# Two channels in one matmul for half of the kernel products, rows of group 2 copied earlier, and six tile stores moved to another queue

## The chip, the cores and the metric

The kernel runs on one core of a Trainium2 chip. A core has five engines with one instruction queue each: TensorE (PE) for matmuls, VectorE (DVE) and GpSimd (POOL) for elementwise work, ScalarE (ACT) for activations and copies, SyncE (SP) for issuing DMAs; ACT and POOL issue DMAs too. Matmuls write to PSUM, everything else lives in SBUF or in DRAM. The metric is the device time of one execution in microseconds, as the median of several runs.

## The reference, cut to what matters

A block of a network over 2048 tokens of 576 channels: a layer norm with modulation, a long convolution over the tokens (S4D), a second layer norm with modulation, and a feed-forward layer of 4608 hidden units. The convolution's filter K is itself computed, from 128 complex modes for each channel:

```
dt = exp(log_dt);  A = -exp(log_A_real) + 1j * A_imag;  C = (C_real + 1j * C_imag) * dt
P  = exp((A * dt)[:, :, None] * pos[None, None, :])
K  = 2 * einsum("dn,dnl->dl", C, P).real
y  = irfft(rfft(u, 2L) * rfft(K, 2L), 2L)[:L] + u * D_skip
x  = x + ga * y(layernorm(x) * (1 + ca) + sa)
x  = x + gb * (relu(h2 @ w1) @ w2),  h2 = layernorm(x) * (1 + cb) + sb
```

`sa, ca, ga, sb, cb, gb` are six vectors of `silu(c) @ w_mod`. All is float32.

## The kernel before, in words

The tokens are taken in four blocks of 512. The feed-forward part (`ffn`) runs block after block and takes most of the time; while PE works on one block there, the filter, the transforms and the norm of the next block are put between its matmuls, from generators. The change lies ahead of the first matmul of `ffn`, where the first block (block 0) is prepared and nothing of the feed-forward part can run yet.

**The filter for block 0.** `KGen.first` computes it in six groups of 96 channels, each group as two halves `u` of 48. The 512 taps are split in 32 positions `j` and 16 offsets `a`: `values` makes a table `W2` over the 32 positions (cosines and sines on ACT, multiplications on DVE and POOL, in `half_values`), `start` makes the first column of `W1`, `doubling` fills its 16 columns in four steps, and `products` multiplies: for each channel one pair of matmuls (real and imaginary part, `r`) with the 128 modes as rows, the 32 positions as weights and the 16 offsets as moving columns. Four channels (`dd`) go to the four strips of 32 PSUM partitions; 48 channels and 2 parts make 96 matmuls for each half, 192 for each group. A float32 matmul stands in the trace as two records, so a group has 384 of them (L264). `powers` makes the factors `Z` that the doubling uses.

**Rows.** `rows(g)` copies a group's products from PSUM to `ke` (one ACT copy of 128 x 384); after three groups `store` writes `ke` to DRAM (`kd`), and `load_kt` reads it back in another layout (`kt`). Group 2 completes the first half of the channels (p = 0), group 5 the second (p = 1). `src_K` adds `D_skip` to the first tap, on one partition of `kt` (on DVE for p = 0, on POOL for p = 1).

**What orders the work.** A scheduler orders each engine's queue at build time, by program order and readiness. Instructions that go through `act` and `pool` of `KGen` (all of its ACT work and nearly all of its POOL work), and through `kept` once `pinned` is set, keep their program order on their engine. In `first` the loop over `g in (0, 2)` has: `raw` (exponentials and turns), doubling and products of groups g and g+1, values of group g+2, then values of group g+3, between the two halves of which `rows(g)` and the first two doubling steps of group g+2 run. After the loop the generator hands over to `conv0` and is taken up again from there for groups 4 and 5.

**The transforms of block 0.** `conv0` has, in this order: the transform of the input half p = 0 (`ZU`, 8 matmuls of 288 columns), the transform of the filter half p = 0 (`ZK`) interleaved with the products of group 4, the doubling and products of group 5, then on DVE the butterflies of U and K, the product Y and the first inverse butterfly V; on PE meanwhile the transform of the input half p = 1, then inverse transforms (L1025), the transform of the filter half p = 1 (`transform1`, L801 and L803, which does the first butterfly on PE with negated constants in 16 matmuls), and the modulation products; then Y and the inverse for p = 1, the norm, and `ffn`. `early` holds the transform constants `fcu` and `fck`; `fcU`, `fcK` and `gc` are tiles of 4 KB a partition in pools that open when those of the first stage close.

**Stores for later blocks.** `W1`, `W2` and `Z` of each half group are also stored to DRAM, for the taps of the later blocks. `values` and `double` issue these on SP, except for group 5 and for `W1` of group 4: those are put in `k.held` and issued on POOL in `conv0`, two behind the load of the modulation weights for sb and cb (L1180), the other six behind that for gb (L1225). Each `W2` tile has 128 x 3072 floats, each `W1` tile 128 x 1536, each `Z` tile 128 x 192.

## Time and profile before

| | us |
|---|---|
| median of 3 runs | 1343.76 |
| lowest and highest | 1338.28 and 1344.12 |
| the profiled execution | 1342.5 |
| its span, first to last instruction | 1340.7 |

| engine | busy us | share of the span |
|---|---|---|
| PE | 1218.8 | 91% |
| DVE | 869.8 | 65% |
| ACT | 504.2 | 38% |
| POOL | 195.2 | 15% |

The profile is one execution. A timeline row has the start and the length in us, the engine (PE for matmuls, PEld for weight loads, SPq for the queue of SP), the line of the kernel, the operation, the written tile and the read ones, partitions x elements, how many instructions were merged, and in brackets how long the engine had been idle before and what released it ("issue" where it waited for nothing that the profile shows). A row of the windows has the length of the stretch, the busy time of each engine with its number of instructions, TensorE's granted clock (1.00 is full), the share of time that the DMA engines were busy, and GB/s. A row of the chain of waits has the start, the length and what the end was waiting for. Durations of merged rows run from the first start to the last end.

### The profile page before, as it was taken

What the parts mean: (1) busy time and instruction counts of PE and PEld (TensorE: products, weight loads), DVE (VectorE), ACT (ScalarE), POOL (GpSimd) and SP (SyncE); (2) the same over time, 40 slices, a digit from 0 to 9 for tenths busy, and PEclk for the clock granted to TensorE, in tenths of its full rate; (3) what the DMA queues carried; (4) which work ended last, traced back from release to release, by engine and by line L of the source; (5) the groups of instructions that cost most, each with busy time, mean ns of one, the idle gap of its engine ahead of it and who ended that gap; (6) DMA issues with size and microseconds to landing.
All of it is one profiled execution on the core that took longest, in us unless ns stands there. A gap on an engine that the chain in (4) does not pass through costs nothing.

```text
span 1340.7 us, 26038 instructions
## 1 busy us (share of the span) xinstructions
PE 1218.8 (91%) x10608; PEld 972.3 (73%) x10608; DVE 869.8 (65%) x1351; ACT 504.2 (38%) x1014; POOL 195.2 (15%) x271
## 2 busy tenths in 40 slices
PE   5125699899999998999999999999999999999998
PEld 3124567678787786777777786787888888888886
DVE  5998898999887898289447885366988222111111
ACT  7987124222224323522243225343322353232331
POOL 1788131111120000111101100100010000000000
PEclk9555799899999998999999999999999999999999
DMA  6666499888898876698779893758997556666651
GB/s 199 246 248 248 145 362 407 303 281 302 293 357 283 291 253 209 222 384 309 245 255 332 289 372 117 264 182 275 318 348 237 169 178 213 196 199 200 196 168 62
DMA packets 132424, 340.47 MB, mean 254 GB/s; under 512 B 22352, under 2 KB 22672, under 8 KB 132304
## 3 DMA queue, kind: packets, MB, share of 16 engines
q1 hardware_dynamic: 105200, 215.21, 48.7%
q0 software_dynamic: 26816, 123.01, 25.1%
q8 instruction: 83, 1.36, 0.4%
q10 hardware_dynamic: 288, 0.59, 0.1%
q14 instruction: 37, 0.30, 0.1%
HBM read 258.55 MB, written 80.22 MB: 253 GB/s over the span
## 4 chain that ended last, share of the span: by engine, by line
PE 71%; DVE 12%; DMA 8%; issue 6%; POOL 2%; ACT 2%; SPq 0%; DVEq 0%; ACTq 0%; POOLq 0%
PE hps L1334 28%; PE acc L1359 27%; PE kps L445 5%; PE ps_f L764 3%; DVE T L515 3%; DVE Y L515 3%; DMA Ua<-Ud 3%; PE kps L264 2%; PE ps_i L1025 2%; DVE W L515 1%; PE kps L612 1%; DMA Ka<-Rd 1%; DMA Zr<-Zd 1%; DMA wm_gb<-in_w_mod_dram 1%; POOL W L59 1%
## 5 line engine op out<-in xcount | busy, mean ns | idle before, releaser
L1359 PE MATMUL acc<-hh,w 128*128 128x512 f32 x1296 | 422.2, 400 | 2.1 <-DVE w L515 2.0
L1334 PE MATMUL hps<-xh,w 128*128 128x512 f32 x1152 | 395.0, 403 | 0.7 <-ACT xh L1090 0.4
L1359 PEld LDWEIGHTS acc<-hh,w 128*128 128x128 f32 x1296 | 243.4, 189 | 55.3 <-DVE w L515 2.8
L1359 PE MATMUL acc<-hl,w 128*128 128x512 f32 x720 | 281.1, 400 | 0.0
L1340 DVE SCALAR_TENSOR_TENSOR hl<-hps,hh 128x512 fp32r<-128x512 f32 x144 | 98.9, 687 | 278.1 <-ACT hh L1339 277.8
L1334 PEld LDWEIGHTS hps<-xh,w 128*128 128x128 f32 x1152 | 218.1, 190 | 48.6 <-ACT xh L1090 1.8
L1334 PE MATMUL hps<-xl,w 128*128 128x512 f32 x576 | 230.7, 401 | 0.2 <-DVE xl L1095 0.2
L1339 ACT ACTIVATE hh<-hps 128x512 fp32r<-128x512 f32 x144 | 86.2, 598 | 328.4 <-PE hps L1334 323.8
L1312 ACT ACTIVATE w<-r 128x576 fp32r<-128x576 f32 x144 | 98.8, 687 | 237.8 <-issue 183.1
L1359 PEld LDWEIGHTS acc<-hl,w 128*128 128x128 f32 x720 | 135.8, 189 | 28.3
L1334 PEld LDWEIGHTS hps<-xl,w 128*128 128x128 f32 x576 | 109.4, 190 | 25.1 <-DVE xl L1095 1.5
L1305 ACT ACTIVATE w<-r 128x640 fp32r<-128x640 f32 x142 | 103.9, 732 | 16.7 <-DMA r<-in_w_dram 15.9
L264 PE MATMUL kps<-W,W 128*32 128x16 f32 x2304 | 40.1, 217 | 76.0 <-POOL W L59 46.9
L1334 PE MATMUL hps<-xs,w 128*128 128x512 f32 x288 | 97.7, 419 | 2.2 <-DVE hl L1340 2.0
L264 PEld LDWEIGHTS kps<-W,W 128*32 128x32 f32 x2304 | 37.7, 150 | 80.5 <-POOL W L59 48.1
L515 DVE TENSOR_TENSOR Y<-Y,T 128x1152 f32<-128x1152 f32 x64 | 85.0, 1352 | 0.1
L445 PEld LDWEIGHTS kps<-W1r,W2r 128*32 128x32 f32 x3456 | 63.8, 146 | 27.9 <-issue 21.6
L445 PE MATMUL kps<-W1r,W2r 128*32 128x48 f32 (+2 forms) x3456 | 71.3, 237 | 8.4 <-issue 7.3
L765 ACT ACTIVATE Z<-ps_f 128x288 f32<-128x288 f32 x104 | 42.4, 408 | 64.5 <-PE ps_f L764 62.3
L1334 PEld LDWEIGHTS hps<-xs,w 128*128 128x128 f32 x288 | 53.7, 192 | 15.0 <-DVE hl L1340 3.1
L515 DVE TENSOR_TENSOR W<-Z 128x576 f32<-128x576 f32 x52 | 37.0, 754 | 40.6 <-ACT Z L765 40.6
L515 DVE TENSOR_TENSOR w<-r,w 128x512 fp32r<-128x512 f32 (+2 forms) x108 | 58.0, 573 | 3.3 <-ACT w L1312 3.0
(215 smaller groups left out, 1361.9 us busy)
## 6 DMA issues: line engine op xcount, KB each, us to landing
r<-in_w_dram SPq DMA_DIRECT2D x144, 320.0 KB, 4.1
r<-in_w_dram SPq DMA_DIRECT2D x144, 288.0 KB, 3.7
w<-L1d SPq DMA_DIRECT2D x108, 320.0 KB, 3.0
w<-L2d SPq DMA_DIRECT2D x108, 288.0 KB, 3.1
W2r<-W2d POOLq DMA_DIRECT2D x18, 1536.0 KB, 9.2
W2d<-W SPq DMA_DIRECT2D x10, 1536.0 KB, 7.4
W<-W1d POOLq DMA_DIRECT2D x18, 768.0 KB, 9.2
Ua<-Ud POOLq DMA_DIRECT2D x12, 1152.0 KB, 10.4
```

Source lines behind the costliest of these rows:

```text
L264: self.nc.tensor.matmul(ps[32 * dd : 32 * dd + 32, 12 * u + q, :], W2[:, r, :, ch], W1[:, u, :, r, ch], start=(r == 0), stop=(r == 1),)
L445: nc.tensor.matmul(ps[32 * dd : 32 * dd + 32, q, :], W2[:, r, :, ch], W1[:, :na, r, ch], start=(r == 1), stop=(r == 0),)
L515: return self.kept(self.nc.vector.tensor_tensor(*args, **kw))
L764: kept(nc.tensor.matmul(o, fc[:, n2, c, :], src(n2), start=True, stop=True))
L765: nc.scalar.activation(Z[:, n2, c], ps[:, :PC], AF.Copy)
L1025: self.nc.tensor.matmul(ps[:, :PC], a, b, start=(i == 0), stop=(i == len(todo) - 1))
L1305: nc.scalar.activation(w[:, 0], r, AF.Copy)
L1312: nc.scalar.activation(w[:, 0:D], r2[g], AF.Copy)
L1334: nc.tensor.matmul(ps, a, x, start=(i == 0), stop=(i == 13))
L1339: nc.scalar.activation(hh, ps, AF.Relu)
L1340: nc.vector.scalar_tensor_tensor(hl, ps, 0.0, hh, op0=ALU.max, op1=ALU.subtract)
L1359: nc.tensor.matmul(acc[i], a, x, start=(f == 0 and j in (0, 3, 6, 9, 12)), stop=(f == NF - 1 and j in (2, 5, 8, 11, 13)),)
```

## The change

- **Products of groups 3 to 5** go through a new method, `pairs`: one matmul takes two channels (`x`), so 64 weight columns (32 positions of two channels) and 32 moving columns (16 offsets of two channels). Of the four blocks that come out, the two that mix channels are not used. A group has 96 matmuls in place of 192 and fills both PSUM banks. `rows` copies each half on its own, and `ke` gets a second plane for the channel of the pair; the rows that belong together lie on every fourth partition, and the store of p = 1 becomes four DMAs, two each on SP and ACT.
- **Rows of group 2** are copied and stored inside the values of group 4 (`ahead`), together with the loads of `fcu` and `fck`; the products of group 3 come behind the values of group 4. `kt` for p = 0 (`kt0`) is loaded inside the values of group 5 (`head`), into the slot of `cc`.
- **Stores.** Those of `W2` and `Z` of group 4 come behind that load, and the six held stores at hand after the doubling of group 4 (`W2` and `Z` of group 5, `W1` of group 4) are issued on SP there; only the two of `W1` of group 5 are left for POOL.
- **Skip addition.** `D_skip` is laid out in a tile `skip` by three small DMAs at the start and added to `ke` before the store, in place of `kt` after the load.
- **U transform for p = 0**: `transform1` with negated constants (`fcUn`, a new load on SP into `fcU`) in place of `transform` and `butterfly1`.
- **Places**: `gcn`, `cb` and `row` go into unused halves of `fcK` and `fcU`.

```diff
--- before.py
+++ after.py
@@ -83,9 +83,15 @@
         self.a, self.th = (self.pa.tile([P, D], F32, name=n) for n in ("lar", "th"))
         ai = self.pt.tile([P, D], F32, tag="T1", bufs=2, name="ai")
         dt = self.pt.tile([P, D], F32, tag="T0", bufs=2, name="dt")
-        self.cc = pc.tile([P, 2, D], F32, name="cc")
+        self.cc = pc.tile([P, 2, D], F32, tag="cc", bufs=1, name="cc")
         self.halfpi = pc.tile([P, 1], F32, name="halfpi")
         nc.vector.memset(self.halfpi, math.pi / 2)
+        self.skip = pc.tile([P, 2, 72], F32, name="skip")
+        nc.gpsimd.memset(self.skip, 0.0)
+        dv = I["dsk"].rearrange("(dd p q) -> p dd q", dd=4, p=2)
+        nc.gpsimd.dma_start(out=self.skip[::32, 0], in_=dv[0])
+        for x in range(2):
+            nc.gpsimd.dma_start(out=self.skip[x::64, 1], in_=dv[1, 2 * x : 2 * x + 2])
         nc.sync.dma_start(out=dt, in_=I["ldt"].unsqueeze(0).to_broadcast([P, D]))
         nc.scalar.dma_start(out=ai, in_=I["ai"])
         nc.scalar.dma_start(out=self.a, in_=I["lar"])
@@ -270,6 +276,26 @@
                         )
                     )
 
+    def pairs(self, banks, W1, W2s, between):
+
+        for u in range(2):
+            a = W2s[u].rearrange("p r j (x c) -> p r (j x) c", x=2)
+            b = W1[:, u].rearrange("p a r (x c) -> p r c x a", x=2)
+            for q in range(12):
+                if q % 6 == 3:
+                    for _ in range(2):
+                        next(between, None)
+                for r in range(2):
+                    for half in range(2):
+                        c = 12 * half + q
+                        o = banks[u][64 * half : 64 * half + 64, 32 * q : 32 * q + 32]
+                        self.mm = self.kept(
+                            self.nc.tensor.matmul(
+                                o.rearrange("p (x a) -> p x a", x=2), a[:, r, :, c], b[:, r, c],
+                                start=(r == 0), stop=(r == 1),
+                            )
+                        )
+
     def first(self, setup, mod, norm):
 
         nc, k = self.nc, self.k
@@ -306,15 +332,22 @@
             self.half_values(g, W2, E[2:4], F[0], True)
             then()
             self.half_values(g, W2, E[0:2], F[1], False)
+            if g != 4:
+                saves(g, 0)
+            self.powers(g, E[4], F[2])
+            if g != 4:
+                saves(g, 1)
+
+        def saves(g, i):
             for u in range(2):
-                save(
-                    strips(k.W2d[2 * g + u], 4),
-                    W2[u].rearrange("p r (y b) c -> p (r y) (b c)", y=2), g == NG - 1,
-                )
-            self.powers(g, E[4], F[2])
-            zs = self.Z[g][1]
-            for u in range(2):
-                save(k.Zd[2 * g + u], zs[:, :, :, u * H : u * H + H], g == NG - 1)
+                if i:
+                    zs = self.Z[g][1]
+                    save(k.Zd[2 * g + u], zs[:, :, :, u * H : u * H + H], g == NG - 1)
+                else:
+                    save(
+                        strips(k.W2d[2 * g + u], 4),
+                        W2s[g][u].rearrange("p r (y b) c -> p (r y) (b c)", y=2), g == NG - 1,
+                    )
 
         def double(g, steps=range(4)):
             self.doubling(g, steps)
@@ -328,17 +361,58 @@
 
         def multiply(g, between=iter(())):
             self.kept = k.kept if g == NG - 2 else lambda x: x
+            if g > 2:
+                kps[g] = [self.bank() for _ in range(2)]
+                self.pairs(kps[g], self.W1[g], W2s[g], between)
+                return
             kps[g] = self.bank()[:, :384].rearrange("p (q a) -> p q a", a=16)
             for u in range(2):
                 self.products(kps[g], self.W1[g], W2s[g][u], u, between)
 
         def rows(g):
             if g % 3 == 0:
-                ke[0] = self.pc.tile([P, 16, 72], F32, tag="ke", bufs=1, name=f"ke_{g}")
-            qs = slice(24 * (g % 3), 24 * (g % 3) + 24)
-            self.act(ke[0][:, :, qs], kps.pop(g).rearrange("p q a -> p a q"), AF.Copy)
-            if g % 3 == 2:
-                self.store(0, g // 3, ke[0].rearrange("p a q -> p (a q)"), nc.sync)
+                ke[0] = self.pc.tile([P, 2, 16, 72], F32, tag="ke", bufs=1, name=f"ke_{g}")
+            t = ke[0]
+            q0 = 24 * (g % 3)
+            if g < 3:
+                self.act(t[:, 0, :, q0 : q0 + 24], kps.pop(g).rearrange("p q a -> p a q"), AF.Copy)
+            else:
+                for u, ps in enumerate(kps.pop(g)):
+                    self.act(
+                        t[:, :, :, q0 + 12 * u : q0 + 12 * u + 12],
+                        ps[:, :384].rearrange("p (q x a) -> p x a q", x=2, a=16), AF.Copy,
+                    )
+            if g == 2:
+                nc.vector.tensor_tensor(t[:, 0, 0], t[:, 0, 0], self.skip[:, 0], op=ALU.add)
+                self.store(0, 0, t[:, 0].rearrange("p a q -> p (a q)"), nc.sync)
+            elif g == 5:
+                nc.gpsimd.tensor_tensor(
+                    t[:, :, 0], t[:, :, 0],
+                    self.skip[:, 1].unsqueeze(1).broadcast_to([P, 2, 72]), op=ALU.add,
+                )
+                f = t.rearrange("p x a q -> p x (a q)")
+                for y in range(2):
+                    for x, eng in enumerate((nc.sync, nc.scalar)):
+                        k.kept(eng.dma_start(
+                            out=k.kd[0][1][64 * y + 32 * x : 64 * y + 32 * x + 32],
+                            in_=f[2 * y + x :: 4, x],
+                        ))
+
+        def ahead():
+            rows(2)
+            t = k.early = self.pc.tile([P, 2, 4, 2, P], F32, tag="W1", bufs=4, name="early")
+            for i, n in enumerate(("fcu", "fck")):
+                nc.sync.dma_start(out=t[:, i], in_=k.I[n])
+
+        def head(g):
+            if g == 0:
+                rows(0)
+            double(g + 2, range(2))
+            if g == 2:
+                k.kt0 = self.pc.tile([P, 16, 72], F32, tag="cc", bufs=1, name="kt0")
+                nc.sync.dma_start(out=k.kt0, in_=k.kd_rows(0, 0))
+                for i in range(2):
+                    saves(4, i)
 
         load, stats, scale, center, affine = norm
         next(mod)
@@ -352,28 +426,31 @@
         values(1, lambda: None)
         for g in (0, 2):
             raw(g // 2 + 1)
-            for i in (g, g + 1):
-                double(i, range(2, 4) if i == 2 else range(4))
-                multiply(i)
-            values(g + 2, lambda: None)
-            if g == 2:
-                t = k.early = self.pc.tile([P, 2, 4, 2, P], F32, tag="W1", bufs=4, name="early")
-                for i, n in enumerate(("fcu", "fck")):
-                    nc.sync.dma_start(out=t[:, i], in_=k.I[n])
-            values(g + 3, lambda: (rows(g), double(g + 2, range(2))))
+            double(g, range(2, 4) if g else range(4))
+            multiply(g)
+            double(g + 1)
+            if g == 0:
+                multiply(1)
+            values(g + 2, ahead if g else lambda: None)
+            if g:
+                multiply(3)
+            values(g + 3, lambda: head(g))
             rows(g + 1)
             if g == 0:
                 for i in (2, 3):
                     affine(i)
         yield
         double(4, range(2, 4))
+        for dst, src in k.held:
+            k.kept(nc.sync.dma_start(out=dst, in_=src))
+        k.held.clear()
         between = yield
         multiply(4, between)
         yield
         double(5)
         yield
+        rows(4)
         multiply(5)
-        rows(4)
         rows(5)
 
     def store(self, s, p, ke, eng):
@@ -615,7 +692,9 @@
 
         nc, act = self.nc, lambda *a, **kw: self.kept(self.nc.scalar.activation(*a, **kw))
         cv = self.cv
-        cb = cv.tile([P, 5, 32], F32, name="cb")
+        spare = self.fcU[:, 2:].rearrange("p a b c -> p (a b c)")
+        cb = spare[:, : 5 * 32].rearrange("p (k r) -> p k r", k=5)
+        row = spare[:, 256:]
         self.kept(nc.vector.tensor_copy(cb, self.ct.unsqueeze(2).broadcast_to([P, 5, 32])))
         ws = {}
 
@@ -643,7 +722,6 @@
                 load(5, "gb")
             elif nm == "gb":
                 yield
-            row = cv.tile([P, 2 * P], F32, tag="row", bufs=1, name=f"row_{nm}")
             act(row[:, 0:P], ps[:, 0:P], AF.Copy)
             for o in (P, P + 64):
                 act(row[0:32, o : o + 64], ps[0:32, P : P + 64], AF.Copy)
@@ -1111,10 +1189,8 @@
         cpsa = self.cps, self.nps = self.pool(c, "cpsa", space=PSUM), 2
         cpsa = cpsa[0]
         self.half_tag = "kt"
-        self.dsk = self.fcU[0:1].rearrange("p a b c -> p (a b c)")[:, :D]
-        nc.gpsimd.dma_start(out=self.dsk, in_=I["dsk"].unsqueeze(0))
-        fcKn = self.fcK.rearrange("p a b c -> p (a b) c")[:, 0:4]
-        gcn = cva.tile([P, 4, P], F32, name="gcn")
+        fcUn, fcKn = (t.rearrange("p a b c -> p (a b) c")[:, 0:4] for t in (self.fcU, self.fcK))
+        gcn = self.fcK.rearrange("p a b c -> p (a b) c")[:, 4:]
         self.pinned = True
 
         def behind(d, op):
@@ -1128,18 +1204,16 @@
             return self.kept(nc.sync.dma_start(out=t, in_=a))
 
         early = self.early
-        kt = [self.load_kt(0, 0)]
+        load(fcUn, I["neg"][2])
+        kt = [self.kt0]
         hv = self.h.rearrange("m n (dd p q) -> m n dd p q", dd=4, p=2)
 
         def src_K(p):
             ktv = kt[p].rearrange("p (t dd g) q -> p t dd g q", t=2, g=2)
-            dv = self.dsk.rearrange("o (dd p q) -> o dd p q", dd=4, p=2)[:, :, p]
-            add = nc.gpsimd.tensor_tensor if p else self.v
-            add(ktv[0:1, 0, :, 0], ktv[0:1, 0, :, 0], dv, op=ALU.add)
             return lambda n2: ktv[:, n2 // 2, :, n2 % 2]
 
-        ZU, ZK = S(0, "ZU"), S(1, "ZK")
-        run(self.transform(lambda n2: hv[:, n2, :, 0], early[:, 0], ZU))
+        WU, ZK = S(2, "WU"), S(1, "ZK")
+        run(self.transform1(lambda n2: hv[:, n2, :, 0], early[:, 0], fcUn, WU))
         next(first)
         ZKs = self.transform(src_K(0), early[:, 1], ZK, self.kept)
         first.send(ZKs)
@@ -1149,10 +1223,8 @@
             behind(d, kg.mm)
         next(first)
         kg.factors.close()
-        W = S(2, "W")
-        run(self.butterfly1(ZU, W))
         U0 = S(0, "U0")
-        run(self.butterfly2(W, U0, -1))
+        run(self.butterfly2(WU, U0, -1))
         self.save(self.Ud[0][0], U0)
         W = S(3, "W")
         run(self.butterfly1(ZK, W))
@@ -1261,13 +1333,13 @@
         self.pinned = False
         self.half_tag = "T"
 
+    def kd_rows(self, s, p):
+        kd = self.kd[s][p]
+        return bass.AP(tensor=kd.tensor, offset=kd.offset, ap=[[72, P], [9216, 16], [1, 72]])
+
     def load_kt(self, s, p):
         kt = self.cv.tile([P, 16, 72], F32, tag="kt", bufs=1 if s else 2, name="kt")
-        kd = self.kd[s][p]
-        d = (self.nc.gpsimd if s else self.nc.sync).dma_start(
-            out=kt,
-            in_=bass.AP(tensor=kd.tensor, offset=kd.offset, ap=[[72, P], [9216, 16], [1, 72]]),
-        )
+        d = (self.nc.gpsimd if s else self.nc.sync).dma_start(out=kt, in_=self.kd_rows(s, p))
         if s == 0:
             self.ktd = self.kept(d)
         return kt
@@ -1565,7 +1637,8 @@
     r["gc"] = (np.stack([np.cos(ps), -np.sin(ps)], axis=2) / 512).astype(np.float32)
     r["neg"] = -np.stack(
         [r["fck"][:, 2:].reshape(P, 4, P),
-         np.stack([r["gc"][:, n, c] for n, c in ((1, 0), (2, 0), (2, 1), (3, 1))], axis=1)]
+         np.stack([r["gc"][:, n, c] for n, c in ((1, 0), (2, 0), (2, 1), (3, 1))], axis=1),
+         r["fcu"][:, 2:].reshape(P, 4, P)]
     )
     sg = 1.0 - 2.0 * (j % 2)
     r["sgn"] = np.stack([sg, -sg], axis=1).astype(np.float32)
```

## The prediction

> **What bounds the kernel now.** I read the windows first, to see where TensorE is full.
>
> ```profile
> core 0: us, PE busy (x) PEld busy (x) DVE busy (x) ACT busy (x) POOL busy (x), PEclk, DMA share, GB/s
> ...
> 150.00:200.00 50.00, 41.05 (x631) 31.44 (x625) 47.57 (x74) 12.63 (x32) 13.62 (x17) 0.90 0.88 320
> ...
> 350.00:400.00 50.00, 50.00 (x913) 40.96 (x912) 39.13 (x60) 13.00 (x27) 10.92 (x17) 1.00 0.87 316
> ...
> 1200.00:1250.00 50.00, 50.00 (x222) 41.38 (x222) 5.54 (x8) 15.15 (x24) 0.00 (x0) 1.00 0.66 198
> ```
>
> From 350 us on PE has work nearly all the time at full clock, and the change leaves the feed-forward part alone. So the end is the moment at which that part starts plus a constant, and a microsecond won ahead of it is a microsecond of the whole. The timeline gives its first matmul.
>
> ```profile
> 209.46 1.20 PE L1334 MATMUL hps<-xs,w 128*128 128x512 f32 x2
> ```
>
> The diff works between 100 and 200 us. There I followed DVE in the timeline, since from 150 on it is busy 47.57 of 50 us.
>
> ```profile
> 129.96 3.54 DVE L515 TENSOR_TENSOR T<-W,Zp 128x768 f32<-128x768 f32 x4
> 138.66 0.45 DVE L515 TENSOR_TENSOR kt<-kt,fcU 1x288 f32<-1x288 f32 x1 [5.16 <-DMA kt<-kd]
> 139.03 0.34 DVE L515 TENSOR_TENSOR t<-W,Zp 128x192 f32<-128x192 f32 x1
> ...
> 149.79 2.76 DVE L515 TENSOR_TENSOR W<-ZU 128x576 f32<-128x576 f32 x4
> 152.58 2.90 DVE L515 TENSOR_TENSOR U<-W 128x576 f32<-128x576 f32 x6
> 155.40 2.76 DVE L515 TENSOR_TENSOR W<-ZK 128x576 f32<-128x576 f32 x4
> ...
> 168.99 2.77 DVE L515 TENSOR_TENSOR V<-Y 128x576 f32<-128x576 f32 x4
> ```
>
> From 138.66 to 171.8 DVE runs almost without a pause: skip addition, doubling of group 5 (139.03 to 149.8), butterflies of U and K, product, V. The 5.16 us ahead of it are a wait for the load of `kt`: a load that is late, not an engine that is full. The chain of waits agrees; it stays on DVE until V and hands over to PE there.
>
> ```profile
> 171.14 3.18 PE ps_i L1025 x12
> ```
>
> The load is late because its store is late: SP stores `kd` only at 125.53, behind four tile stores and `fck`.
>
> ```profile
> 112.14 0.88 SPq L362 DMA_DIRECT2D early<-in_fcu_dram  x1
> 117.72 2.36 SPq L298 DMA_DIRECT2D W2d<-W  x2
> 120.86 2.56 SPq L298 DMA_DIRECT2D Zd<-zs  x2
> 123.47 1.97 SPq L362 DMA_DIRECT2D early<-in_fck_dram  x1
> 125.53 1.97 SPq L382 DMA_DIRECT2D kd<-ke  x2
> ```
>
> **The change, part by part.** *Rows of group 2 forward.* The rows are PE's, ACT's, DVE's and POOL's in the timeline, then the landing times of `kd`, then two windows.
>
> ```profile
> 109.63 2.15 PE L264 MATMUL kps<-W,W 128*32 128x16 f32 x127 [1.83 <-issue]
> ...
> 125.42 1.80 PE L264 MATMUL kps<-W,W 128*32 128x16 f32 x99 [4.62 <-issue]
> ```
> ```profile
> 112.32 0.92 ACT L56 ACTIVATE c<-c,halfpi 128x768 f32<-128x768 f32 x1
> ...
> 125.47 0.44 ACT L56 ACTIVATE zs<-c,halfpi 128x192 f32<-128x192 f32 x1
> ```
> ```profile
> 120.44 0.34 DVE L180 TENSOR_TENSOR tc<-cc,s 128x192 f32<-128x192 f32 x1
> ```
> ```profile
> 115.68 1.85 POOL L59 TENSOR_TENSOR W<-c,E 128x384 f32<-128x384 f32 x2
> ...
> 128.68 1.15 POOL L59 TENSOR_TENSOR zs<-zs,E 128x192 f32<-128x192 f32 x2
> ```
> ```profile
> DMA to landing us min/median/max: 3.6/5.0/6.9
> ```
> ```profile
> 110.00:120.00 10.00, 5.25 (x334) 5.03 (x329) 6.93 (x20) 7.60 (x15) 10.00 (x15) 0.50 0.73 269
> 120.00:130.00 10.00, 5.38 (x159) 4.14 (x152) 9.48 (x28) 5.17 (x11) 10.00 (x16) 0.56 1.00 350
> ```
>
> The products of group 2 end near 111.3, 98 records into the burst of 109.63. Copied and stored at once, `kd` is in memory by about 118. `kt0` takes the slot of `cc`, whose last reader runs at 120.44, so it is issued near 121.5 and there by 127, over 11 us ahead of 138.66. The 5.16 us go, and what is late next is DVE itself, at 133.5 after its four T. The ACT copy now stands in ACT's fixed order inside group 4's values and waits for 111.3; queued behind it are abs, two sines and the cosine that POOL uses at 115.68 (done at 113.2). I estimate 1.2 us of delay, hidden by POOL's own queue, full from 110 to 130; without that cover it costs up to 1.2.
>
> *Skip addition.* The 0.45 us on DVE go. Two additions over 128 partitions come, one on DVE between 110 and 120 (busy 6.93 of 10), one on POOL (0.57 us by the zs row) in the path to `kt1`. POOL's old 2.08 us at 173 lay beside PE. The memset and the three small loads stand at the start, where POOL idles.
>
> *U transform.* It now does the first butterfly too: 32 matmul records for 16, and the 2.76 us of DVE go.
>
> ```profile
> 127.16 5.83 PE L764 MATMUL ps_f<-h,early 128*128 128x288 f32 x16
> ```
> ```profile
> 174.31 0.48 PE ps_f L801 x2
> ```
>
> Between 16 records in 5.83 us at this place and 0.24 us each in the K1 transform, 32 cost 7.8 to 11.7; I take 9.5, in the middle. PE starts about 126, when ACT's last reading of the factor tiles under the target ends (125.47 + 0.44), and is done at 135.5.
>
> *Paired products.* A group costs 192 records in place of 384. Unpaired ones start every 17 ns (127 in 2.15 us), and after some 128 PE stands still for 1.8 to 4.6 us waiting for nothing that the profile shows, which I read as instructions not yet there: a block each 4.0 us. A paired record has 64 weight and 32 moving columns; no row shows it.
>
> ```profile
> 237.65 2.31 PE L445 MATMUL kps<-W1r,W2r 128*32 128x48 f32 x96
> ```
> ```profile
> 143.00 1.24 PE L764 MATMUL ps_f<-kt,early 128*128 128x288 f32 x4
> ...
> 162.93 0.42 PE L264 MATMUL kps<-W,W 128*32 128x16 f32 x6 [2.12 <-issue]
> ```
> ```profile
> 173.22 2.08 POOL L1138 TENSOR_TENSOR kt<-kt,fcU 1x288 f32<-1x288 f32 x1 [11.07 <-DMA kt<-kd]
> ```
>
> Below it are the 17 ns; the nearest row, 32 weight and 48 moving columns, has 24 ns, and two of those, 48 ns, do more than one paired record, so that is the upper end. I take 30 ns, 5.8 us a group, nearer to the row than to its double, and keep both ends.
>
> [...]
>
> Group 4 with the K transform in it: 5.8 + 4 times 1.24 + some 0.5 for switching = 11.3 us, from 135.5 to 146.8, K's last copy near 146.5. DVE doubles group 5 from 133.5 (10.8 us as before) to 144.3 and makes U0 until 147.1. So K is there in time, by half a microsecond. Group 5: 5.8 us and one standstill of 2 to 154.6. Before, products ended at 163.35 and `kt1` came 9.9 us later; with POOL's addition 10.5, so 165.1. The K1 transform, at 174.3 before, could start 8.4 earlier, at 165.9. That just fits too. The second ACT copy of a group adds 0.48 us where ACT is a quarter busy.
>
> *Six stores moved.* Two W2 tiles (1.6 MB each), two Z tiles and two W1 tiles (0.8 MB each) leave POOL, where they were issued from 177 to 199, for SP after 129. 4.9 MB at the 350 GB/s of 120 to 130 last 14 us. The W1 stores wait for POOL's doubling of group 4; queued behind them are constants that wait for the products of group 4 anyway, then half of the `kd` rows, `kt1` and x, none due before 150. On POOL the stores stood around the load for gb, and PE waited for it.
>
> ```profile
> PE kps L445 <- issue: 4.3, 3, 2.5
> ...
> PE mps_gb L638 <- DMA wm_gb<-in_w_mod_dram: 0.5, 1, 0.5
> ```
>
> They also ran beside loads at the head of the feed-forward part; PE loses a few microseconds there, by these waits of 200 to 330 with other causes, so I count zero and keep 3 us either way.
>
> **Sum.** 5.16 + 0.45 + 2.76 = 8.4 us on DVE's chain, 0.5 at gb, less 0.9 for the two fits without slack: 8.0. The profiled execution took 1342.5 us (span 1340.7 and 1.8 around it), 1.3 below the median 1343.76 and inside the runs. 1342.5 - 8.0 = **1334.5 us**.
>
> **Rivals.** *The U transform waits.* Its negated constants are new on SP. Queued behind group 4's stores, which start near 122 and take 9.5 us for 3.3 MB, they land at 133, not 126: U ends at 142, K at 153.5, and DVE's 155.40 becomes 153.9. Gain 1.5 + 0.5: 1340.5 us. For: SP issued `fck` behind just these stores. Against: their tile lies on inputs that are read last near 104, and `fcu` went ahead of the stores.
>
> *Paired records cost more.* At the upper end, 48 ns, groups 4 and 5 cost 9.2 us each, but a block then lasts longer than the 4.0 us in which one comes, and the standstill goes: products end at 159.4, `kt1` comes at 169.9, 4.0 later than it could be used: 1342.5 - 8.9 + 4.0 = 1338 us. [...]
>
> *Slower: PE starves beside the stores.* The longest standstill, 4.62 us, fell where W2 stores ran and DMA was full. Now 4.9 MB run beside groups 4 and 5. U late by 6.5, two standstills 2.6 us longer and 384 records at 48 ns (6.9 us) move the end of products from 154.6 to 173.2, `kt1` to 183.7, 9.4 behind 174.3: 1352 us. It is slower than before once products end after 164, by over 0.5% from 170.5.
>
> *It moves nothing*, since the queues keep their order: 1342.5. *More than forecast*: DVE's wait for products of group 3 goes as well (1.9) and the head of the feed-forward part loses 3 less: 1329.
>
> ```profile
> 119.50 0.56 DVE L173 TENSOR_TENSOR W<-s,E 128x384 f32<-128x384 f32 x1 [1.93 <-PE kps L264]
> ```
>
> **How the numbers follow.** Forecast 0.46 (1331 to 1337), more 0.12, late U 0.20, dear pairs 0.14, nothing 0.03, starved PE 0.05. About 0.5%, 6.7 us, is what a measurement of this kernel can tell from no change: faster is below 1337.0, slower above 1350.5. Faster: 0.46 + 0.12 + 0.02 of the dear pairs = 0.60; slower 0.05; same 0.35. The range goes from 1327 (more, with 2 us of spread) to 1342.5 (late U with 2 us); the starved case and the tails are left out.
>
> **What would show it.** Right: no DVE wait on `kt`; U0's butterfly starts by 145; V ends near 163.5; `kt1` lands by 166; the first L1334 matmul is at 201.5, not 209.46. Late U: PE pauses inside the U transform for a load of `fcU`. Dear pairs: 192 records last over 8 us without a standstill. Starved: standstills over 4 us from 135 to 155. I am wrong as a whole if the feed-forward part starts 8 us earlier and the end does not follow.

## The result, and the profile after

| | median, us | lowest to highest | runs | ratio to before, 95% interval |
|---|---|---|---|---|
| before | 1341.24 | 1338.28 to 1344.12 | 8 | 1 |
| after | 1352.74 | 1345.30 to 1357.54 | 8 | 1.0078 [1.0052, 1.0103] |

The change makes the kernel slower; 1334.5 us was forecast, with 1327.0 to 1342.5 as the range. The profiled execution of after took 1351.98 us (span 1350.2).

The timeline of after on PE, around the changed work (start, duration, engine, line, names, shape, count, in brackets the idle time ahead and its releaser). Its lines moved: L293 holds the paired products, L270 the unpaired ones, L879 and L881 the transform with the first butterfly, L842 the K transform, L1406 the feed-forward part.

```profile
112.22 12.38 PE L293 MATMUL kps<-W,W 128*64 128x32 f32 x192
...
133.95 0.45 PE L293 MATMUL kps<-W,W 128*64 128x32 f32 x4 [3.41 <-POOL W L59]
134.91 1.48 PE L293 MATMUL kps<-W,W 128*64 128x32 f32 x20 [0.52 <-POOL W L59]
136.32 2.29 PE L881 MATMUL ps_f<-h,fcU 128*128 128x288 f32 x4
...
143.43 0.65 PE L881 MATMUL ps_f<-h,fcU 128*128 128x288 f32 x2
...
145.26 3.24 PE L293 MATMUL kps<-W,W 128*64 128x32 f32 x48
148.43 2.24 PE L842 MATMUL ps_f<-kt,early 128*128 128x288 f32 x4
150.60 3.26 PE L293 MATMUL kps<-W,W 128*64 128x32 f32 x48
...
164.33 12.38 PE L293 MATMUL kps<-W,W 128*64 128x32 f32 x192
...
188.47 0.72 PE L879 MATMUL ps_f<-kt,early 128*128 128x288 f32 x2 [3.02 <-DMA kt<-kd]
...
224.39 0.73 PE L1406 MATMUL hps<-xs,w 128*128 128x512 f32 x2 [0.29 <-DVE xs L1171]
```

A group of 192 paired records lasts 12.38 us: 64.5 ns a record, where the forecast took 30 and its upper bound was 48. No `issue` stands between them, so the standstills have gone; the records fill the time instead. The price is the same at both clocks: 48 records take 3.24 us from 145.26 and 3.26 us from 150.60, where the windows (busy time by engine, then the granted clock, DMA share and GB/s) give 1.00 and 0.50:

```profile
145.30:148.30 3.00, 3.00 (x49) 3.00 (x48) 2.80 (x6) 0.41 (x1) 0.60 (x1) 1.00 0.52 176
...
150.70:153.70 3.00, 3.00 (x48) 3.00 (x48) 1.43 (x2) 0.41 (x1) 0.00 (x0) 0.50 0.71 272
```

The four K transform records between them do follow the clock: 1.24 us at a granted clock of 1.00 in before (from 143.00), 2.24 at 0.50 here (from 148.43).

The groups of instructions by line and shape from 100 to 200 us say the same in one row each (busy time, mean ns of one record from its start to its end, which overlaps its neighbours, idle time by releaser). Before, then after:

```profile
L264 PE MATMUL kps<-W,W 128*32 128x16 f32 x1536 | 27.0, 216 | 35.9 <-issue 18.7 <-POOL W L59 17.2
```
```profile
L293 PE MATMUL kps<-W,W 128*64 128x32 f32 x576 | 38.2, 313 | 3.9 <-POOL W L59 3.9
...
L270 PE MATMUL kps<-W,W 128*32 128x16 f32 x384 | 6.7, 220 | 19.5 <-POOL W L59 16.5 <-issue 2.9
```

384 unpaired records of group 2 cost 6.7 us of work in after, so the 1152 of groups 3 to 5 in before cost 27.0 - 6.7 = 20.3 us of work and 18.7 - 2.9 = 15.8 us of standstill: 36.1. The 576 paired ones cost 38.2 and no standstill. Halving the number of records bought nothing.

DVE's timeline shows who waits:

```profile
145.21 2.89 DVE L592 TENSOR_TENSOR U<-WU 128x576 f32<-128x576 f32 x6
151.15 1.43 DVE L592 TENSOR_TENSOR W<-ZK 128x576 f32<-128x576 f32 x2 [3.05 <-ACT ZK L843]
161.96 1.43 DVE L592 TENSOR_TENSOR W<-ZK 128x576 f32<-128x576 f32 x2 [9.39 <-ACT ZK L843]
...
174.22 2.77 DVE L592 TENSOR_TENSOR V<-Y 128x576 f32<-128x576 f32 x4
```

The wait for `kt` is gone, and U's second butterfly starts at 145.21, as forecast. Then DVE stands 12.4 us for the K transform, which PE works on between the products of group 4. V is done at 177.0 instead of 171.8.

SP's timeline has the second cause, and the view of the DMA issues from 110 to 150 us (size, time from issue to landing) says when it took effect:

```profile
114.21 1.70 SPq L459 DMA_DIRECT2D kd<-ke  x2
...
120.75 0.38 SPq L413 DMA_DIRECT2D kt<-kd  x1
121.21 3.51 SPq L324 DMA_DIRECT2D W2d<-W  x2
124.81 2.84 SPq L324 DMA_DIRECT2D Zd<-zs  x2
127.70 2.95 SPq L1204 DMA_DIRECT2D fcU<-in_neg_dram  x1
```
```profile
fcU<-in_neg_dram SPq DMA_DIRECT2D x1, 256.0 KB, 7.1
```

The negated constants of the U transform are issued at 127.70, behind group 4's stores, and land 7.1 us later, at 134.8. PE did what it could without them, stood, did the first 24 products of group 4 from 133.95 and read the constants at 136.32. The trace puts the stand of 3.41 us on POOL's `W`, since these 24 products stand ahead of the constants' first use in PE's queue; that the constants are the cause is shown by e3 below, where they come early and the U transform runs through until 135.4. Here it was done at 144.1.

### The profile page after: what moved, and what is told of

Its sections match the earlier page's. It is cut to its first block, busy times and chain, and to the rows that moved or that the text cites. A ratio compares the mean times of both kernels' runs of the same rounds, so it can differ in the third digit from the quotient of the medians.

```text
span 1350.2 us, 24940 instructions
## 1 busy us (share of the span) xinstructions
PE 1243.9 (92%) x10048; PEld 993.8 (74%) x10048; DVE 867.3 (64%) x1347; ACT 504.8 (37%) x1017; POOL 190.7 (14%) x268
## 4 chain that ended last, share of the span: by engine, by line
PE 76%; DVE 11%; DMA 4%; issue 4%; ACT 2%; POOL 2%; SPq 0%; ACTq 0%; DVEq 0%; POOLq 0%
PE hps L1406 30%; PE acc L1431 29%; PE kps L522 5%; PE ps_f L842 5%; PE kps L293 2%; POOL W L59 2%; DVE T L592 2%; PE ps_i L1103 1%; DVE Y L592 1%; PE kps L689 1%; DMA Ka<-Rd 1%; DMA Ua<-Ud 1%; DVE k L140 1%; DMA L1d<-w 1%; DVE T L255 1%
## 5 line engine op out<-in xcount | busy, mean ns | idle before, releaser
L1406 PE MATMUL hps<-xh,w 128*128 128x512 f32 x1152 | 394.0, 402 | 0.5 <-ACT xh L1168 0.4
L1406 PEld LDWEIGHTS hps<-xh,w 128*128 128x128 f32 x1152 | 217.1, 189 | 48.2 <-ACT xh L1168 2.3
L1406 PE MATMUL hps<-xl,w 128*128 128x512 f32 x576 | 230.5, 400 | 0.4 <-DVE xl L1173 0.4
L1406 PEld LDWEIGHTS hps<-xl,w 128*128 128x128 f32 x576 | 109.0, 189 | 25.5 <-DVE xl L1173 2.3
L1406 PE MATMUL hps<-xs,w 128*128 128x512 f32 x288 | 96.2, 414 | 2.5 <-DVE hl L1412 2.0
L592 DVE TENSOR_TENSOR Y<-Y,T 128x1152 f32<-128x1152 f32 x64 | 85.0, 1352 | 0.1
L270 PE MATMUL kps<-W,W 128*32 128x16 f32 x1152 | 19.9, 218 | 59.4 <-POOL W L59 46.2
L1406 PEld LDWEIGHTS hps<-xs,w 128*128 128x128 f32 x288 | 52.9, 189 | 15.5 <-DVE hl L1412 3.3
L270 PEld LDWEIGHTS kps<-W,W 128*32 128x32 f32 x1152 | 18.7, 150 | 60.9 <-POOL W L59 47.0
```

The costliest lines, as they stand in the source:

```text
L270: self.nc.tensor.matmul(ps[32 * dd : 32 * dd + 32, 12 * u + q, :], W2[:, r, :, ch], W1[:, u, :, r, ch], start=(r == 0), stop=(r == 1),)
L592: return self.kept(self.nc.vector.tensor_tensor(*args, **kw))
L1406: nc.tensor.matmul(ps, a, x, start=(i == 0), stop=(i == 13))
```

## The experiments

Times are medians, the ratio is to before in the same batch (1341.2 to 1343.0 us, 16 to 21 runs each; 8 for after). The probes e5, e8 and e15 ran once each: of them only the lengths of records are read, not the times. In these three, and in e12 and e13, the products of groups 3 to 5 read other weights than the filter needs, so that half of K is not the reference's; they show times alone.

### The two suspects undone, and done alone

Theory: the paired records (64.5 ns) and the late constants each cost time. Rivals: the moved stores, or one cause alone. e1 is after with the products unpaired:

```diff
-            if g > 2:
-                kps[g] = [self.bank() for _ in range(2)]
-                self.pairs(kps[g], self.W1[g], W2s[g], between)
-                return
...
-                for u, ps in enumerate(kps.pop(g)):
-                    self.act(t[:, :, :, q0 + 12 * u : q0 + 12 * u + 12], ...)
+            self.act(t[:, 0, :, q0 : q0 + 24], kps.pop(g).rearrange("p q a -> p a q"), AF.Copy)
```

> The changed kernel with the products of groups 3 to 5 unpaired again, 384 records a group; all else as changed. Theory A (a paired record costs 64 ns whatever the clock, and the stream of them lets the granted clock fall to 0.5, which doubles the K transform between them): a quarter of group 4 with two K outputs takes 1.7 + 1.3 us again, not 3.2 + 2.2; the last K output comes near 155.5 instead of 161.5, the products end near 171 instead of 176.7, and the time falls by about 6 us, to 1347. Rival B (the late load of the negated constants alone makes it slow, the pairs only fill the pause): no change, 1352. Rival C (the six stores on SP starve PE): standstills over 4 us in the products between 145 and 170, time up, above 1355.

e2 is before with the change's own lines on `pairs`, on `multiply`, on `rows` with its copies and stores, and on the places of `cb`, `row` and `gcn`, and nothing else of it:

> The kernel before with the pairs in groups 3 to 5 and nothing else of the change but places (gcn, cb and row in unused parts of fcK and fcU, to make room for the second plane of ke) and the rows of the pairs. A: group 4 with the K transform takes 4 times 5.4 instead of 2.9 us, group 5 12.4 and not 13.6 with standstills; K's butterfly moves from 155.4 to about 161, the products end near 173 instead of 163.4, the time rises by 8 to 12 us, to about 1351. B: within 2 us of before, 1341. C: as B.

e3 is after with the constants loaded beside `fcu`, ahead of the stores; e4 is e1 and e3 together:

```diff
-            t = k.early = self.pc.tile([P, 2, 4, 2, P], F32, tag="W1", bufs=4, name="early")
+            t = k.early = self.pc.tile([P, 3, 4, 2, P], F32, tag="W1", bufs=4, name="early")
...
+            n = t[:, 2].rearrange("p a b c -> p (a b) c")[:, 0:4]
+            nc.sync.dma_start(out=n, in_=k.I["neg"][2])
...
-        load(fcUn, I["neg"][2])
```

> The changed kernel with the negated constants of the U transform loaded with fcu and fck into the unused third of their tile, ahead of group 4's stores. The pause of the U transform (130.5 to 136.3) goes. B: U ends near 136 instead of 144.4, everything behind follows by 8 us, and the time is within 3 us of 1342. A: the same 8 us on PE up to the end of the products, since PE is the bound there; K's last output near 154, products' end near 169; time near 1345, because the pairs stay dear. C: no gain, the stores still run beside the products.

> Both: unpaired products and the early negated constants, the rest as changed. A with B adding up: K's last output near 148, DVE without a wait of over 1 us from 134 to 163, products' end near 162, the first matmul of the feed-forward part 3 to 6 us ahead of 209.5; time 1333 to 1337, below before. If C holds too, standstills of over 4 us beside the stores and a time at or above 1341.

| | products | constants | us | ratio, 95% interval |
|---|---|---|---|---|
| after | paired | late | 1352.74 | 1.0078 [1.0052, 1.0103] |
| e1 | unpaired | late | 1341.10 | 1.0016 [0.9992, 1.0040] |
| e3 | paired | early | 1342.81 | 1.0005 [0.9988, 1.0022] |
| e4 | unpaired | early | 1334.35 | 0.9950 [0.9933, 0.9968] |
| e2, before with pairs | paired | none needed | 1350.74 | 1.0058 [1.0038, 1.0079] |

Unpairing wins 0.6% in either row, pairing alone costs 0.6%, and early constants win 0.7% in either row. Both causes are real and add up; with both taken out the rest of the change is worth 0.5%, 6.7 us. The times of e2 and e4 came as theory A said. e1 came out 6 us below the 1347 of theory A, and e3 below its 1345, in the range of rival B (late constants alone): it takes the runs together to show both causes.

### What makes a paired record dear

e5 gives each group other operands, each in a helper of its own, so that each has its own line:

```diff
+    def narrow_moving(...):   # group 3
+        matmul(o, a[:, r, :, c], b[:, r, c, 0], ...)
+    def narrow_weights(...):  # group 4
+        matmul(o, a[:, r, 0:32, c], b[:, r, c], ...)
+    def contiguous(...):      # group 5
+        matmul(o, w[:, 64 * c : 64 * c + 64], m[:, 64 * c + 32 * r : 64 * c + 32 * r + 32], ...)
```

> Changed kernel with other operands in the products of groups 3 to 5, so rows 72 to 143 of each K tile are not those of the reference: group 3 keeps 64 weight columns with 16 moving ones, group 4 takes 32 weight columns with 32 moving ones, group 5 keeps 64 with 32 but reads its weights and moving values from contiguous columns. A paired record lasted 64.5 ns. If the weight load of 64 columns sets it, groups 3 and 5 stay at 60 to 65 ns and group 4 falls to 25 or less. If the 32 moving columns set it, group 3 falls to 30 or less and group 4 stays at 60. If the strided reading sets it, group 5 alone falls to 30. [...]

```profile
112.37 12.35 PE L300 MATMUL kps<-W,W 128*64 128x16 f32 x192
...
142.68 1.04 PE L305 MATMUL kps<-W,W 128*32 128x32 f32 x48
...
151.32 3.22 PE L311 MATMUL kps<-W,W 128*64 128x32 f32 x102
```

Half the moving columns change nothing (64.3 ns), half the weight columns bring 21.7 ns, and 64 weight columns in a row 31.6: it takes two conditions together, a wide weight load and spaced columns. e8 takes the two operands apart (24 values between neighbours means 96 bytes):

> Changed kernel with other operands in the products of groups 3 to 5 (rows 72 to 143 of each K tile are not those of the reference), 64 weight and 32 moving columns in all three: in group 3 the weight columns lie 24 values apart as in the change and the moving ones in a row, in group 4 the weights in a row and the moving ones apart as in the change, in group 5 the weights 2 values apart. The record with both in a row took 31.6 ns in e5. If the spacing of the weights decides: group 3 64 ns, group 4 32 ns, and group 5 says whether any spacing costs (64) or only a wide one (32 to 40). If the spacing of the moving columns decides: group 3 32 ns, groups 4 and 5 64 ns.

```profile
114.86 12.37 PE L302 MATMUL kps<-W,W 128*64 128x32 f32 x190 [0.58 <-ACT ke L56]
...
146.62 1.61 PE L306 MATMUL kps<-W,W 128*64 128x32 f32 x48
...
156.28 6.00 PE L310 MATMUL kps<-W,W 128*64 128x32 f32 x192
```

Spaced weights take 65 ns, weights in a row with spaced moving columns 33.5, weights 2 values apart 31.3. In both probes group 3 ran at a granted clock of 0.50 and the other rows shown at 1.00, but the spaced record of after has its price at both clocks. So the weights' spacing decides, and 8 bytes are still free. e15 looks for the limit:

> The change with the negated constants early, and with the 64 weight columns of a product 8 values apart in group 3, 4 apart in group 4 and 3 apart in group 5 (rows 72 to 143 of each K tile are not the reference's). In e8 columns 2 apart took 31 ns a record and 24 apart 65 ns. If the price grows with the distance: 33 to 45 ns at 3 and 4 apart, 45 to 60 at 8 apart. If there is one limit between 2 and 24 apart: every group at either 31 to 36 or 62 to 68 ns. [...]

```profile
111.07 12.35 PE L301 MATMUL kps<-W,W 128*64 128x32 f32 x192
...
141.52 3.08 PE L305 MATMUL kps<-W,W 128*64 128x32 f32 x48
...
153.43 5.53 PE L309 MATMUL kps<-W,W 128*64 128x32 f32 x100
```

8 apart 64.3 ns, 4 apart 64.2, 3 apart 55.3, all at a granted clock of 0.50 by the windows. In a row at that clock a record takes 55.0 ns (163 in 8.96 us in e13 below). So at this clock 3 apart costs no more than in a row, 4 apart has the whole price, and a larger distance adds nothing: 8 apart is level with 4, and the 24 apart of after, 64.5 ns, as well. So there is a limit at this clock, between 3 and 4 values. What sets it is not shown, and 3 apart was not run at the full clock.

### The forecast's chain with both prices put right

e12 is the change with one edit in the products, by which the 64 weights of a record are read in a row; e13 has early constants besides:

```diff
-            a = W2s[u].rearrange("p r j (x c) -> p r (j x) c", x=2)
+            a = W2s[u].rearrange("p r j c -> p r (j c)")
...
-                                o.rearrange("p (x a) -> p x a", x=2), a[:, r, :, c], b[:, r, c],
+                                o.rearrange("p (x a) -> p x a", x=2), a[:, r, 64 * c : 64 * c + 64], b[:, r, c],
```

> The change with one edit: the products of groups 3 to 5 read their 64 weight columns in a row instead of 24 values apart (rows 72 to 143 of each K tile are not the reference's). Everything else, the late constants too, as in the change. If the price of a record is what failed and the late constants hide behind DVE's doubling of group 5: 1333 to 1338. If the late constants cost 5 us or more by themselves, as e11 against e10 and e3 against the change say: 1340 to 1346.

> As e12, with the negated constants of the U transform loaded early: the change with both misjudged prices put right and nothing else (rows 72 to 143 not the reference's). If the forecast's chain holds apart from these two: U transform done by 136, products of group 5 done by 156 to 159, first feed-forward matmul at 202 to 205, time 1329 to 1335, at or below e4's 1334.4. If another wait takes the place (DMA traffic of the moved stores, the load of kt, x): first feed-forward matmul at 207 to 210 and 1334 to 1338.

e12 took 1336.84 us, 0.9957 [0.9941, 0.9972]; e13 1334.12, 0.9928 [0.9908, 0.9948]. Against after, the spacing of the weights alone is worth 1.2%, some 16 us, more than unpairing. With short records the late constants cost 0.3%, and the two intervals overlap. e13 on PE:

```profile
116.95 8.96 PE L293 MATMUL kps<-W,W 128*64 128x32 f32 x163 [1.14 <-issue]
125.84 1.33 PE L880 MATMUL ps_f<-h,early 128*128 128x288 f32 x2
...
146.75 4.22 PE L293 MATMUL kps<-W,W 128*64 128x32 f32 x124
...
151.58 2.93 PE L293 MATMUL kps<-W,W 128*64 128x32 f32 x92
...
164.51 5.59 PE L1104 MATMUL ps_i<-V,gc 128*128 128x288 f32 x12 [4.51 <-DVE V L593]
169.93 1.13 PE L1104 MATMUL ps_i<-V,fcK 128*128 128x288 f32 x4
170.90 0.65 PE L880 MATMUL ps_f<-kt,early 128*128 128x288 f32 x2
...
204.89 0.73 PE L1408 MATMUL hps<-xs,w 128*128 128x512 f32 x2 [0.29 <-DVE xs L1172]
```

The U transform starts at 125.84 and group 5 ends at 154.5. The K1 transform no longer waits for `kt`; it stands behind the inverse transform, which waits 4.51 us for V. The bound is DVE again, as the forecast had it.

### The moved stores

e6 is e4 with the six stores back on POOL, as below; e7 is before with these three lines alone put in at the same place:

```diff
-        for dst, src in k.held:
-            k.kept(nc.sync.dma_start(out=dst, in_=src))
-        k.held.clear()
```

> Unpaired products, negated constants of the U transform loaded early, and the six tile stores back on POOL where the kernel before has them (the kernel of e4_unpaired_early without the move of the stores). If the move of the stores carries e4's gain, by a shorter head of the feed-forward part: first feed-forward matmul at 205 to 209, the part from there to the end 1131, time 1339 to 1342, no gain over before. If the gain came from the rows of group 2 and the U transform: the part from there to the end stays at 1122, time 1331 to 1335. Products of group 5 should lose their longest standstill (4.68 us) if that is the stores' doing.

> The kernel before with one edit: the six tile stores issued on SP behind the doubling of group 4. If they carry the gain: part from the first feed-forward matmul to the end 1121 to 1126 instead of 1131.2, its start 209 to 214, time 1332 to 1337. If their move is worth nothing, as the prediction counted: 1339 to 1343.

e6 took 1337.28 us, 0.9966 [0.9944, 0.9988]; e7 1342.46, 1.0019 [1.0001, 1.0037]. e6 lies between its two expected ranges, its interval overlaps with e4's, and e7 gains nothing: that the move carries e4's gain is not borne out. The guess had come from single profiles: from the first feed-forward matmul to the end e4's took 1121.7 us, before's 1131.2. But e7's profile, too, took 1124.1, and its median is no better than before's. That part has 7932 to 7935 matmul records in the eleven kernels whose windows were taken there, and it took from 1120.6 to 1135.6 us, one profile each, as the windows of before, e1 and e11 show:

```profile
209.46:1340.70 1131.24, 1107.25 (x7934) 886.73 (x7932) 693.30 (x935) 371.28 (x662) 89.66 (x128) 0.99 0.75 255
```
```profile
219.51:1340.10 1120.59, 1102.72 (x7932) 883.61 (x7932) 693.28 (x935) 371.70 (x662) 86.66 (x124) 0.99 0.75 256
```
```profile
221.18:1356.80 1135.62, 1101.04 (x7932) 878.70 (x7932) 693.74 (x935) 370.90 (x662) 86.63 (x124) 0.98 0.75 252
```

What sets this scatter is open. It means that a gain of 5 us is not read from one profile's end.

### Complete versions with weights in a row

e9 is e4 with the W2 tiles laid out with the powers innermost and the two channels of a pair beside each other; e10 pairs again on this layout; e11 is e10 with late constants; e14 is e10 with the layout in groups 3 to 5 alone and the second K rows stored in eight pieces.

```diff
-                self.pw.tile([P, 2, 32, H], F32, tag="W2", bufs=5, name=f"W2_{2 * g + u}")
+                self.pw.tile([P, 2, H // 2, 2, 32], F32, tag="W2", bufs=5, name=f"W2_{2 * g + u}")
...
+            W2 = [w.rearrange("p r c x j -> p r j x c") for w in W2s[g]]
```

> The kernel of e4_unpaired_early (products unpaired, negated constants early) with the W2 tiles laid out so that the 32 or 64 weight columns of a product lie in a row; DVE pays for it with 4 more instructions a group. If weights in a row are read faster at 32 columns too: records of groups 0 to 5 and of the feed-forward part's K products fall below 16.8 and 24 ns; if the spacing only matters at 64 columns, they stay. Standstills after 128 records stay in any case. Time 1332 to 1337 (e4: 1334.4); above 1340 the strided writes of DVE and POOL cost more than thought.

> As e9_layout, and the products of groups 3 to 5 paired again, with 64 weight columns in a row; the rows are copied block by block on ACT. This has every part of the change with the two misjudged prices put right: records near 31 ns instead of 64.5 and no wait for the negated constants. If the forecast's chain holds apart from these two: U transform done by 136, products of group 5 done by 156 to 159, first feed-forward matmul 203 to 206, time 1328 to 1335. If pairing gives nothing even then, because another wait takes its place: like e4, 1334 to 1336, with the feed-forward part starting at 208 or 209.

> As e10_contig, with the negated constants of the U transform where the change has them, behind the stores of group 4. If the late constants have a price of their own: 3 to 8 us above e10, with PE waiting for fcU in the U transform. If with short records the delay is hidden (DVE's doubling of group 5 ends at 145 anyway): within 2 us of e10.

> A complete version with weights in a row in groups 3 to 5 alone, early constants, rows copied block by block, and the second K rows stored in eight pieces of 16 rows each instead of e10's four with a split row index. If the slow store was e10's trouble: kt lands by 172 instead of 184, time 1332 to 1337. If the strided writes of DVE and POOL cost the gain: U transform starts 2 to 4 us later than in e4 and the time stays at 1337 to 1342. It beats e4 (0.995 of before) only if it falls below 1333.

e9 took 1335.36 us, 0.9945 [0.9923, 0.9966], level with e4: its unpaired records fall from 17.5 ns (96 in 1.68 us in e4) to 12 (96 in 1.15 us), at a granted clock of 1.00 and 0.97 in the 10 us around them, but 21.2 us of standstills stay. e10 took 1348.65, 1.0055 [1.0033, 1.0077], a miss, and its cause is my own edit. SP and PE of e10, two timelines:

```profile
161.89 1.24 SPq L399 DMA_DIRECT2D kd<-ke  x2
179.69 0.38 SPq L1344 DMA_DIRECT2D kt<-kd  x1
```
```profile
184.06 1.30 PE L880 MATMUL ps_f<-kt,early 128*128 128x288 f32 x2 [11.91 <-DMA kt<-kd]
```

Four stores of 144 KB, whose target I wrote with an outermost dimension of 2, took 17.8 us until `kt` could be issued; in e13 the same bytes took 6.3 (155.88 to 162.23), and in e14, in eight pieces of 16 rows each, 8.1 (161.05 to 169.15). For e10 the windows give a DMA share of 0.12 and 46 GB/s from 170 to 180, where e13 has 0.93 and 354 GB/s from 157 to 162. So the slow transfer goes with the form of the store; how the form makes it slow is not shown. e11 took 1353.71, 1.0083 [1.0054, 1.0112], with the same fault. e14, with the store mended, took 1334.73, 0.9950 [0.9931, 0.9969]: a complete kernel that beats before, level with e4. In its profile the U transform waits 5.0 us for DVE, whose 128x384 writes into the new layout take 0.81 us instead of e4's 0.55; that this gives back what short records win is likely, and wasn't tried alone. e4, e9 and e14 are the best complete versions run, and their intervals do not part them.

## Why the prediction was wrong, point by point

**The step that failed** is the price of a paired record: "two of those, 48 ns, do more than one paired record, so that is the upper end". It measured 64.5 ns. The bound counted columns and forgot how they lie in memory. The row it rests on has spaced columns too, but 32 of them, and two such loads are not one of 64: narrowed to 32 columns the record took 21.7 ns (e5). Why the wider load costs three times as much wasn't tried. With weights in a row the 30 ns taken are nearly right at full clock, 31 to 34; at a granted clock of 0.50 such a record takes 55. So the idea of pairing was sound and its layout was not.

**Late U** came true as well: the constants landed at 134.8 (133 in the rival), U was done at 144.1 (142). I gave it a chance of 0.20 and argued it away by the place of `fcu`, but the code has the constants behind the stores on the same queue, and that order decided. Two rivals held at once. I priced them together only inside the "starved" case; its 1352 us is near the result for another reason, since no standstill lay among the paired records at all.

**Right, as after and e13 show it.** Rows forward: `kd` stored at 114.21, `kt` issued at 120.75, no wait for it on DVE. U transform: 9.5 us forecast, 10.1 in e13. Group 5's products were to end at 154.6, and ended at 154.5 in e13, or 151.4 without the shift named next. ACT's copy waited 2.60 us for the products of group 2; POOL, busy all 20 us from 110 to 130, hid it. The six stores at zero: e7 is 0.0 to 0.4% slower than before, and e6 and e4 overlap.

**A shift that is not the change's.** In e13 V ended at 166.4, not 163.5, and the first feed-forward matmul came at 204.89, not 201.5. But e13's profile lies 3.1 us behind that of before already in the products of group 2, ahead of the changed work. Before, then e13 on PE and on DVE:

```profile
101.69 2.57 PE L264 MATMUL kps<-W,W 128*32 128x16 f32 x157 [0.66 <-POOL W L59]
```
```profile
104.79 2.57 PE L270 MATMUL kps<-W,W 128*32 128x16 f32 x157 [0.67 <-POOL W L59]
```
```profile
132.78 3.54 DVE L593 TENSOR_TENSOR T<-W,Zp 128x768 f32<-128x768 f32 x4
...
163.70 2.76 DVE L593 TENSOR_TENSOR V<-Y 128x576 f32<-128x576 f32 x4
```

The place moves in other runs too: the burst with the last 98 records of group 2 starts at 109.63 in before, 109.84 in e1, 110.60 in after, 112.74 in e13, and at 111.14 in e2, which leaves the work ahead of it as it is. In after a share of it shows at the first 20 matmuls of the kernel, on the modulation weights, which took 8.27 us there and 7.20 in before. Why they differ, and where the rest of e13's 3.1 us comes from, is open. Without the 3.1 us, DVE's last four T of group 4 start at 129.7 as in before (129.96), V ends at 163.3 and the feed-forward part starts at 201.8: 7.7 us won of 8.0.

**From the start of that part to the end.** The forecast took the end to follow this start microsecond for microsecond. The runs bear that out only roughly. After started the part 14.9 us late and ended 9.5 late. And e4, e9 and e14 start it at 209.03, 212.61 and 210.72, no or little earlier than before's 209.46, with medians 6 to 8 us below before's; e4 had been expected to start it 3 to 6 us earlier. Its first feed-forward matmul:

```profile
209.03 0.74 PE L1389 MATMUL hps<-xs,w 128*128 128x512 f32 x2 [0.29 <-DVE xs L1153]
```

Where these versions win their time is open; one profile each, with the scatter shown above, does not say. In e9 and e14 the layout also reaches K's products in that part, which may be a share of it: PE is busy there for 1093.9 and 1097.7 us, 1107.3 in before. But in e4, without that layout, it is 1100.6.

**What the forecast got for right and wrong.** With its two misjudged prices put right, the change ran at 1334.12 us (a ratio of 0.9928, some 9.6 us less than before), 0.4 us from the 1334.5 forecast. The chain up to the feed-forward part was right to 0.3 us in one profile. That the time agrees as closely is partly luck: e13's six runs lie between 1329.53 and 1336.88, and the step from that start to the end is not shown.

## What to carry to other kernels

Before two small matmuls are merged, look at the distance between neighbouring weight columns in SBUF: here 64 columns cost 31 to 34 ns at up to 2 values apart (full clock) and 64 ns or more from 4 apart (4 and 8 apart at a granted clock of 0.50, 24 apart at both), enough to eat the whole gain of halving the records. Look, too, at what stands ahead of a new small load on its queue: here 256 KB put in front of the big stores won 0.7%, and 0.3% with short records, where the intervals overlap. And when two rivals don't exclude each other, price them together.

## What the runs showed of the hardware that was not expected

- A record with 64 weight columns 24 values apart takes 64 to 68 ns at a granted clock of 0.50 and of 1.00 alike, so its price doesn't follow TensorE's clock; with columns in a row it takes 55 and 31 to 34.
- With half the instructions the standstills of groups 3 to 5 all but go: 15.8 us in before, none in after, and 1.1 in e13, whose records take 31 to 55 ns. In after the longer records took back what this saved. That the standstills are instructions not yet there, a block each 4.0 us, was my reading; no run shows it.
- PE was busy all of the 25 us from 150 to 175 in after, at a clock of 0.50; in before it was busy 17.94 us at 0.86. Why the clock fell is not settled: in e3 the same records ran at 1.00 until 150.

```profile
150.00:175.00 25.00, 25.00 (x301) 21.37 (x300) 14.33 (x18) 3.87 (x10) 0.76 (x1) 0.50 0.37 134
```
```profile
150.00:175.00 25.00, 17.94 (x463) 14.52 (x457) 24.79 (x36) 4.51 (x11) 3.34 (x3) 0.86 0.72 239
```
